# Attention, then two expert layers on one core: first q, k and v split before the branch, the attention's order planned anew, weight decoding moved later, one product's sixth block moved to its end

## The chip, the cores and the metric

The kernel runs on one core of one Trainium2 chip. The metric is the device time of one execution in microseconds, taken as the median of several runs.

## The reference, cut to what matters

Attention over 2 batches and 12 heads (448 positions, 64 channels) with a soft cap of the scores, then an expert layer that takes the maximum of three products, then a second one with a leaky rectifier.

```python
scores = cap * tanh((q @ k.T) / sqrt(64) / cap)
attn = exp(scores - max) / (sum + 1e-9)          # 2 x 12 heads, 448 x 448
x = (attn @ v)                                   # 896 tokens x 768
h = maximum(maximum(x @ w1, x @ w2), x @ w3)     # 768 -> 768, three products
y = h @ w_out                                    # 768 -> 768
g = y @ w_in;  g = max(g, 0) + alpha * min(g, 0) # 768 -> 2048
out = g @ w_out2                                 # 2048 -> 768
```

## The kernel before, in words

Every product of the expert layers is made of three matmuls: an operand is split into a high part, rounded to the matmul's short format (fp32r), and a remainder, and high times high, high times low and low times high are summed (`product`, L94 to L100). A split costs a cast (`rounded`, L82 on ACT or L84 on DVE) and a subtraction on DVE (`remainder`, L87). Weights come in a 64-bit format and are decoded by ACT and DVE in five steps (`decoded`, L102): ACT's absolute value (W0), two steps of DVE (W1, W2), ACT's cast (W3), DVE's subtraction (W4).

The attention goes over 12 pairs of heads. A pair has two units, of 4 and of 3 rows of probabilities, so there are units 0 to 23. For unit u TensorE makes two score tiles (`scores`, L252, each 6 or 3 matmuls), ACT takes tanh of each (L270) and exp of the unit (L274), and TensorE multiplies with v (`chunk_weighted`, L292, below PV u). The pairs in `FULL` use the probabilities and v unsplit, in plain fp32; for the others DVE first splits the unit's probabilities (`a_high` AH, `a_low` AL). The column sums come with PV; they are copied by ACT (`taken`, L322), sent over DRAM to invert and spread them, and a pair's result is normalised and split on DVE and ACT into `xh`, `xl`.

The order of all of this on every engine is made at build time: `fast_attention` lists the tasks with an engine, a cost, the tasks they depend on and a key (`KEYS`, L190); `planned` (L150) runs a list schedule over them, and the tasks are issued in the order that it gives and kept in it on each engine (`in_order`). Three weights of the first expert layer are decoded inside the attention, not before the units in `GATES` (L188). The score tiles have two PSUM buffers, so the scores of a tile wait for the tanh of the tile two before it. Engines run their own queue strictly in order.

Ahead of the attention the program loads `cap`, computes a flag from it on DVE, and every engine loads the flag and branches on it (L78, L665). Eleven matmuls on a constant (L76) run before the branch. The loads of the first pair's q and k (`first`, in two column cuts) are issued on SP behind the load of `cap`.

After the attention, `experts` (L535) computes h in six blocks f of 128 features, each with three weights; for f = 0 the last two of the twelve (batch, k) parts, which need the last two pairs, come at the end. Then y (L651 to L657): for each of six blocks o the two batches after one another, each over the six blocks k of h. Then `moe2` (L560): 16 blocks of g, six blocks of the output.

Of the kernel before, what the change touches and what calls it, by code (L numbers as in the profile page):

```python
# [10 lines left out]
F32 = mybir.dt.float32  # L11
# [9 lines left out]
P = 128  # L21
# [9 lines left out]
def attention_moe_moe2(ctx: ExitStack, tc: tile.TileContext, t):  # L31
# [18 lines left out]
    cap_t = const.tile([P, 1], F32, name="cap_t")  # L50
    nc.sync.dma_start(out=cap_t, in_=t["cap"].to_broadcast([P, 1]))
    cap2 = const.tile([P, 1], F32, name="cap2")
    nc.vector.tensor_tensor(out=cap2, in0=cap_t, in1=cap_t, op=ALU.mult)  # L53
    flag = const.tile([P, 1], I32, name="flag")
    nc.vector.tensor_scalar(out=flag, in0=cap2, scalar1=CAP_BOUND * CAP_BOUND, scalar2=None, op0=ALU.is_le)
    s_in = const.tile([P, 1], F32, name="s_in")
    nc.vector.reciprocal(out=s_in, in_=cap_t)
    nc.vector.tensor_scalar(out=s_in, in0=s_in, scalar1=scale, scalar2=None, op0=ALU.mult)
    alpha_t = const.tile([P, KF], F32, name="alpha_t")


    first = const.tile([P, QK], F32, name="first")
    CUT = S + P
    for cols in (slice(0, CUT), slice(CUT, QK)):
        nc.sync.dma_start(out=first[:, cols], in_=t["qk"][0, :, cols])
# [3 lines left out]
    fills = const.tile([P, 2, P], BF16, name="fills")  # L69
    for i in range(2):  # L70
        nc.gpsimd.memset(fills[:, i], float(i))

# [77 lines left out]
    def planned(tasks, start):  # L150
# [36 lines left out]

    GATES = (10, 13, 22)  # L188

    KEYS = dict(  # L190
        Lx=-8, Lv=-6, XKH=-4, XKL=-3.9, VH=-1.5, VL=-1.2, TKA=1.9, TKB=2, INV=2.2, NM=2.7, XH=2.9, XL=3.2,
        SC=-1.4, TA=-0.5, EX=0, AH=0.1, AL=0.2, PV=1.25,
    )
# [3 lines left out]
    def fast_attention(xh, xl, pools, begin):  # L197
# [6 lines left out]
        for i in range(2):  # L204
            sets["h", i] = vpool.tile([P, 4, 4 * D], F32R, name=f"vh{i}")
            sets["l", i] = vpool.tile([P, 4, 4 * D], F32R, name=f"vl{i}")
            if FULL:
                sets["f", i] = vpool.tile([P, 4, 4 * D], F32, name=f"vf{i}")

# [42 lines left out]
        def scores(i):  # L252

            p, block = CHUNKS[i]
            h, l = ops[p]
            sc = ps.tile([P, 2, 512], F32, tag="ps", name="sc")
            k0 = S + (3 if block is None else block) * P
            for m, (k_, q_) in enumerate(((h, h), (h, l), (l, h))):
# [124 lines left out]
        of = [[u for u in range(n // 2) if CHUNKS[2 * u][0] == p] for p in range(PAIRS)]  # L383
        for name in ("KIN", "QIN"):
            add((name, 0), name, 0.3 if name == "KIN" else 1.4, [], 0, lambda: None)
        for i in range(2):
            for part in "hlf" if FULL else "hl":
                add(("ONE", part, i), "Pool", 1.0, [], i, beside, part, i)
        for p in range(PAIRS):
# [4 lines left out]
            if p == 0:  # L394
                for x, (cols, dep) in enumerate(((slice(0, CUT), "KIN"), (slice(CUT, QK), "QIN"))):
                    m = cols.stop - cols.start
                    add(("XKH", 0, x), "DVE", rounding("DVE", m), [((dep, 0), 0.0)], -99 + x, qk_high, 0, cols, "DVE")
                    add(("XKL", 0, x), "DVE", low(m), [("XKH", 0, x)], -98.5 + x, qk_low, 0, cols)
            else:
                transfer(("Lx", p), 0.63, 2.6, past("XKL", p - 2, 0), s0 + KEYS["Lx"], load_qk, p)  # L400
                free = past("SC", 2 * of[p - 2][-1] + 1) if p > 1 else []
                engine, cols = ROUND["QK"], slice(0, QK)
                deps = [(("Lx!", p), 0.9)] + free
# [5 lines left out]
            transfer(("Lv", p), 1.2 if full else 0.63, 2.0, free + (ones if full else []), s0 + KEYS["Lv"], load_v, p)  # L409
            ready_v = [(("Lv!", p), 0.9)]  # L410
            if not full:
# [5 lines left out]
            for u in of[p]:  # L417
                even, m = u % 2 == 0, S * UNITS[u]
                for i in (2 * u, 2 * u + 1):
                    deps = past("SC", i - 1) + past("TA", 2 * u - 2) + past("TA", 2 * u - 1)  # L420
                    deps += [("XKL", 0, 0 if i == 0 else 1)] if p == 0 else [("XKL", p, 0)]
                    cost = 0.71 if CHUNKS[i][1] in (0, 1) else 0.6 if i % 2 == 0 else 0.8
                    add(("SC", i), "PE", cost, deps, u + KEYS["SC"] - i % 2 * 1000, scores, i)
# [11 lines left out]
                if not full:  # L435
# [4 lines left out]
                    add(("AL", u), "DVE", low(m), [("AH", u)] + free, u + KEYS["AL"], a_low, u)  # L440
                cost = (3.1 if even else 2.7) if full else (2.5 if even else 2.25)
                deps = [("EX" if full else "AL", u)] + ready_v + past("PV", u - 1)
# [17 lines left out]
            for h, name in enumerate(("NA", "NB")):  # L460
                add((name, p), "DVE", low(S), [(("DX!", p), 1.4)], s0 + KEYS["NM"], normal, p, h)
            engine = ROUND["X"]
            add(("XH", p), engine, rounding(engine, S), [("NA", p), ("NB", p)], s0 + KEYS["XH"], x_high, p, engine)
            add(("XL", p), "DVE", low(S), [("XH", p)], s0 + KEYS["XL"], x_low, p)
        for w, gate in enumerate(GATES):
            stages = begin(w)
            step = lambda stages=stages: next(stages, None)
            free = [("EX", gate)]
            transfer(("WL", w), 0.4, 4.2, [("EX", max(0, gate - 4))] + past("W2", w - 2), 1000 + w * 10, step)
            times = (("ACT", 0.8), ("DVE", 1.05), ("DVE", 1.8), ("ACT", 0.8), ("DVE", 0.9))  # L470
            for j, (engine, cost) in enumerate(times):
                deps = [(("WL!", w), 0.3)] + free + past("W4", w - 2) if j == 0 else [(f"W{j - 1}", w)]
                add((f"W{j}", w), engine, cost, deps, 1000 + w * 10, step)
        anchors = {}
        for name in planned(tasks, 3.6):
            task, args = tasks[name][4]
            task(*args)
            if name in (("EX", n // 2 - 1), ("AL", splitting[-1]), ("PV", n // 2 - 1), ("DA", PAIRS - 1)):
                anchors[name[0]] = list(nc.cur_bb.bb.instructions)[-1]
# [80 lines left out]
    def moe2(y, gh, gl, wpool, small, accumulator):  # L560
        yh, yl = y
        for f in range(KF):
# [4 lines left out]
            ng = small.tile([P, B, S], F32, tag="m", name="ng")  # L567
# [28 lines left out]
    def whole(fast):  # L596
        tag = "f" if fast else "g"
        with ExitStack() as outer:
# [43 lines left out]
            with ExitStack() as st:  # L642
                small = st.enter_context(tc.tile_pool(name=f"s{tag}", bufs=2))
                late = st.enter_context(tc.tile_pool(name=f"l{tag}", bufs=1))
                for ins in behind:
                    st.enter_context(tc.issue_after(ins))
                hs = [hidden(late, f) for f in range(KD)]
                for f in range(KD):
                    experts(f, weight, xs, hs, accumulator, small, 2 if f == 0 else 0)
                y = tuple(act.tile([P, KD, B, S], F32R, tag=f"a{h}", name=f"y{h}") for h in "hl")  # L650
                for o in range(KD):  # L651
                    wh, wl = whole_weights(wpool, t["w_out"][o])
                    acc = accumulator()
# [77 lines left out]
```

## Time and profile before

| what | value |
|---|---|
| median of 3 runs | 530.16 us (529.76 to 530.53) |
| the profiled execution, its own time | 533.62 us |
| its span, first to last instruction | 532.2 us, so 1.4 us lie around it |
| granted clock of TensorE, mean | 0.994 |
| busy: PE, DVE, ACT | 97%, 70%, 43% of the span |

A busy PE is not PE at its peak: the ends of matmuls are modelled, and spacing between the starts of matmuls says more than busy time. The profiled execution took 3.5 us longer than the median run.

### The profile page before, as it was taken

The numbers are of one execution on the slowest core, as the hardware profiler recorded it, in microseconds if no ns is written. First come the engines' busy times: TensorE is split into PE (matmuls) and PEld (weight loads), VectorE is DVE, ScalarE is ACT, GpSimd is POOL, SyncE is SP. The second block draws the span as 40 slices with busy tenths as digits, with TensorE's granted clock in tenths as the row PEclk, the third lists the DMA queues.
The fourth block names the chain that finished last, engine by engine and source line by source line (L and its number), as shares of the span: only waits on it lengthen the run. The fifth ranks groups of instructions, "written<-read, shape, count | busy, mean of one in ns | idle before, by whom it ended". The sixth has DMA issues, their size and how long they took to land.

```text
span 532.2 us, 6370 instructions
## 1 busy us (share of the span) xinstructions
PE 518.1 (97%) x2511; PEld 442.1 (83%) x2511; DVE 372.1 (70%) x482; ACT 228.9 (43%) x276; POOL 3.9 (1%) x12
## 2 busy tenths in 40 slices
PE   6999899999999999999999999999999999999994
PEld 3566466679999999999999999999999999999993
DVE  3487999748897666857667899999889555555300
ACT  5999989924333323333323433343233223223100
POOL 2000000000000000000000000000000000000000
PEclk9999999999999999999999999999999999999999
DMA  6548343135435323333322332333322354353001
GB/s 184 170 125 223 72 118 97 40 96 161 148 120 177 115 86 103 113 120 118 114 73 112 118 111 73 114 118 110 103 64 101 110 148 135 106 153 121 1 36 41
DMA packets 28262, 59.19 MB, mean 111 GB/s; under 512 B 15424, under 2 KB 18624, under 8 KB 28224
## 3 DMA queue, kind: packets, MB, share of 16 engines
q1 hardware_dynamic: 28224, 58.69, 36.1%
q8 instruction: 22, 0.36, 0.3%
q14 instruction: 16, 0.13, 0.1%
HBM read 55.85 MB, written 2.80 MB: 110 GB/s over the span
## 4 chain that ended last, share of the span: by engine, by line
PE 96%; ACT 1%; DMA 1%; DVE 0%; issue 0%; DVEq 0%; ACTq 0%
PE acc L98 26%; PE acc L99 26%; PE acc L100 26%; PE pv L311 12%; PE sc L261 6%; ACT a L270 1%; DMA cap_t<-in_cap 1%; ACT a L274 0%; ACT e L322 0%; DVE qkl L87 0%; ACT wh L82 0%; DVE qkh L84 0%; ACT ot L584 0%; DVEq L78 0%; DVE cap L53 0%
## 5 line engine op out<-in xcount | busy, mean ns | idle before, releaser
L82 ACT CAST wh<-f 128x768 fp32r<-128x768 f32 (+1 forms) x58 | 47.2, 814 | 203.7 <-PE acc L99 195.4
L87 DVE TENSOR_TENSOR wl<-f,wh 128x768 fp32r<-128x768 f32 (+1 forms) x58 | 53.7, 925 | 52.4 <-ACT wh L82 52.3
L98 PE MATMUL acc<-xh,wh 128*128 128x448 f32 x216 | 79.0, 366 | 0.0
L99 PE MATMUL acc<-xl,wh 128*128 128x448 f32 x216 | 79.0, 366 | 0.0
L100 PE MATMUL acc<-xh,wl 128*128 128x448 f32 x216 | 78.9, 365 | 0.0
L108 ACT ACTIVATE f<-raw 128x768 f32<-128x768 f32 (+1 forms) x58 | 51.2, 882 | 54.2 <-DVE wl L87 39.1
L98 PE MATMUL acc<-yh,wh 128*128 128x448 f32 x192 | 70.7, 368 | 0.0
L99 PE MATMUL acc<-yl,wh 128*128 128x448 f32 x192 | 70.7, 368 | 0.0
L100 PE MATMUL acc<-yh,wl 128*128 128x448 f32 x192 | 70.7, 368 | 0.0
L98 PE MATMUL acc<-gh,wh 128*128 128x448 f32 x192 | 70.7, 368 | 0.0
L99 PE MATMUL acc<-gl,wh 128*128 128x448 f32 x192 | 70.7, 368 | 0.0
L100 PE MATMUL acc<-gh,wl 128*128 128x448 f32 x192 | 70.7, 368 | 0.0
L118 DVE SCALAR_TENSOR_TENSOR f<-raw,f 128x768 int32<-128x768 int32 (+1 forms) x58 | 53.9, 929 | 1.7
L115 DVE SCALAR_TENSOR_TENSOR f<-raw,f 128x768 int32<-128x768 int32 (+1 forms) x58 | 53.9, 929 | 1.5
L110 DVE TENSOR_SCALAR f<-f 128x768 f32<-128x768 f32 (+1 forms) x58 | 31.6, 545 | 22.6 <-ACT f L108 22.6
L270 ACT ACTIVATE a<-sc,s_in 128x896 f32<-128x896 f32 (+1 forms) x48 | 41.9, 919 | 5.5 <-PE sc L261 5.3
L98 PEld LDWEIGHTS acc<-xh,wh 128*128 128x128 f32 x216 | 40.6, 188 | 3.8 <-issue 0.7
L99 PEld LDWEIGHTS acc<-xl,wh 128*128 128x128 f32 x216 | 40.6, 188 | 3.4 <-DVE xl L87 0.2
L100 PEld LDWEIGHTS acc<-xh,wl 128*128 128x128 f32 x216 | 40.6, 188 | 3.2
L311 PE MATMUL pv<-a,vf 128*128 128x448 f32 (+1 forms) x112 | 41.1, 557 | 0.0
L274 ACT ACTIVATE a<-a,cap_t 128x1792 f32<-128x1792 f32 (+3 forms) x28 | 39.5, 1422 | 0.5
L98 PEld LDWEIGHTS acc<-yh,wh 128*128 128x128 f32 x192 | 36.0, 188 | 3.7
(66 smaller groups left out, 725.7 us busy)
## 6 DMA issues: line engine op xcount, KB each, us to landing
raw<-in_w SPq DMA_DIRECT2D x18, 768.0 KB, 4.4
raw<-in_w_in SPq DMA_DIRECT2D x16, 768.0 KB, 4.3
raw<-in_w_out SPq DMA_DIRECT2D x12, 768.0 KB, 4.3
raw<-in_w_out SPq DMA_DIRECT2D x12, 640.0 KB, 4.0
qkd<-in_qk SPq DMA_DIRECT2D x11, 480.0 KB, 4.1
rb<-row SPq DMA_DIRECT2D x24, 112.0 KB, 3.0
out<-ot SPq DMA_DIRECT2D x12, 224.0 KB, 2.8
vf<-in_v SPq DMA_DIRECT2D x14, 128.0 KB, 4.0
```

Source lines behind the costliest of these rows:

```text
L82: nc.scalar.copy(out=hi, in_=src)
L87: nc.vector.tensor_tensor(out=lo, in0=src, in1=hi.bitcast(F32), op=ALU.subtract)
L98: nc.tensor.matmul(out, wh, xh, start=first and i == 0, stop=False)
L99: nc.tensor.matmul(out, wh, xl, start=False, stop=False)
L100: nc.tensor.matmul(out, wl, xh, start=False, stop=last and i == n - 1)
L108: nc.scalar.activation(out=f, in_=high.bitcast(F32), func=AF.Abs)
L115: nc.vector.scalar_tensor_tensor(out=fi, in0=low, scalar=29, in1=fi, op0=ALU.logical_shift_right, op1=ALU.bitwise_or)
L118: nc.vector.scalar_tensor_tensor(out=fi, in0=high, scalar=-0x40000000, in1=fi, op0=ALU.bitwise_and, op1=ALU.bitwise_or)
L261: nc.tensor.matmul(sc[:, head, :S], k_[r, k0 : k0 + P], q_[r, :S], start=m == 0, stop=m == 2)
L270: nc.scalar.activation(out=splits[i // 2][:, at : at + sc.shape[1]], in_=sc, func=AF.Tanh, scale=s_in)
L274: nc.scalar.activation(out=a, in_=a, func=AF.Exp, scale=cap_t)
L311: nc.tensor.matmul(pvs[p][:, head, :S], v_, a_[r, j], start=start, stop=stop)
```

## The change

The part ahead of the branch: `cap` is loaded from ACT's queue, so that the first cut of q and k is the first load on SP; v of the first pair is loaded into a tile of its own there, with its ones written by POOL; and DVE splits the first cut (576 columns) behind the flag's arithmetic and ahead of its own load of the flag.

```diff
-    nc.sync.dma_start(out=cap_t, in_=t["cap"].to_broadcast([P, 1]))
+    nc.scalar.dma_start(out=cap_t, in_=t["cap"].to_broadcast([P, 1]))
+    first = const.tile([P, QK], F32, name="first")
+    CUT = S + P
+    first_parts = [const.tile([P, CUT], F32R, name=f"first{part}") for part in "hl"]
+    first_v = const.tile([P, 4, 4 * D], F32, name="first_v")
+    for cols in (slice(0, CUT), slice(CUT, QK)):
+        nc.sync.dma_start(out=first[:, cols], in_=t["qk"][0, :, cols])
...
+    nc.gpsimd.memset(first_v[:, :, D : 3 * D], 1.0)
+    for h in range(2):
+        nc.sync.dma_start(out=first_v[:, :, 3 * h * D : (3 * h + 1) * D], in_=t["v"][0, :, :, h])
...
     nc.vector.tensor_scalar(out=flag, in0=cap2, scalar1=CAP_BOUND * CAP_BOUND, scalar2=None, op0=ALU.is_le)
+    nc.vector.tensor_copy(out=first_parts[0], in_=first[:, :CUT])
+    nc.vector.tensor_tensor(
+        out=first_parts[1], in0=first[:, :CUT], in1=first_parts[0].bitcast(F32), op=ALU.subtract
+    )
```

The planner: other keys, costs and gates; all that it yields is an order.

```diff
-    GATES = (10, 13, 22)
+    GATES = (10, 16, 23)
-        SC=-1.4, TA=-0.5, EX=0, AH=0.1, AL=0.2, PV=1.25,
+        XH=-2.55, XL=-3.75, SC=-4.5, TA=-0.25, EX=-28.75, AH=-3.0, AL=-12.65, PV=7.5,
-                    cost = 0.71 if CHUNKS[i][1] in (0, 1) else 0.6 if i % 2 == 0 else 0.8
+                    cost = (0.86, 0.8, 0.72, 0.8)[i % 4]
-        for name in planned(tasks, 3.6):
+        for name in planned(tasks, 5.0):
```

The second layer's temporary `ng` lies in the tiles `first` and `first_v` in turn, in place of two buffers of a pool. The first block of y takes k = 0 to 4 of both batches first, and the sixth block of h, k = 5, for both at the end:

```diff
-                    for b in range(B):
-                        terms = [((wh[:, k], wl[:, k]), tuple(h_[:, b] for h_ in hs[k])) for k in range(KD)]
-                        product(acc[:, b], terms)
+                    early = KD - 1 if o == 0 else KD
+                    for k0, k1 in ((0, early), (early, KD)):
+                        for b in range(B) if k0 < k1 else ():
+                            terms = [((wh[:, k], wl[:, k]), tuple(h_[:, b] for h_ in hs[k])) for k in range(k0, k1)]
+                            product(acc[:, b], terms, k0 == 0, k1 == KD)
```

What it moves. First PE at the start of the attention, from score tile 3 (of one head's width, `sc_192`) to PV 0; `sc` are scores, `pv` the product with v, numbers are buffers, `x4` is four matmuls. Before:

```order
L261 MATMUL sc_192<-qkh_145 128x448
L261 MATMUL sc_192<-qkl_146,qkh_145 128x448
L261 MATMUL sc_192<-qkh_145,qkl_146 128x448
L261 MATMUL sc_209<-qkh_181 128x448 x2
L261 MATMUL sc_209<-qkl_182,qkh_181 128x448 x2
L261 MATMUL sc_209<-qkh_181,qkl_182 128x448 x2
L261 MATMUL sc_218<-qkh_181 128x448 x2
L261 MATMUL sc_218<-qkl_182,qkh_181 128x448 x2
L261 MATMUL sc_218<-qkh_181,qkl_182 128x448 x2
L311 MATMUL pv_229<-a_166,vf0_138 128x448 x4
```

and now, up to the first score tile of unit 2 (`sc_220`):

```order
L270 MATMUL sc_196<-firsth_61,qkh_152 128x448
L270 MATMUL sc_196<-firstl_62,qkh_152 128x448
L270 MATMUL sc_196<-firsth_61,qkl_153 128x448
L320 MATMUL pv_202<-a_169,first_v_63 128x448 x4
L270 MATMUL sc_220<-qkh_207 128x448 x2
L270 MATMUL sc_220<-qkl_208,qkh_207 128x448 x2
L270 MATMUL sc_220<-qkh_207,qkl_208 128x448 x2
```

The score tiles 4 and 5 of unit 2 stood ahead of PV 0; now PV 0 comes right behind tile 3. Second, PE in the middle, from score tile 29 (`sc_663`, the second one of unit 14) to the first matmuls of PV 12 (`pv`, pair 6, split). Before:

```order
L261 MATMUL sc_663<-qkh_567 128x448 x2
L261 MATMUL sc_663<-qkl_568,qkh_567 128x448 x2
L261 MATMUL sc_663<-qkh_567,qkl_568 128x448 x2
L261 MATMUL sc_687<-qkh_567 128x448 x2
L261 MATMUL sc_687<-qkl_568,qkh_567 128x448 x2
L261 MATMUL sc_687<-qkh_567,qkl_568 128x448 x2
L261 MATMUL sc_700<-qkh_567 128x448
L261 MATMUL sc_700<-qkl_568,qkh_567 128x448
L261 MATMUL sc_700<-qkh_567,qkl_568 128x448
L311 MATMUL pv_707<-ah_659,vh0_136 128x448
L311 MATMUL pv_707<-al_677,vh0_136 128x448
L311 MATMUL pv_707<-ah_659,vl0_137 128x448
```

and now:

```order
L270 MATMUL sc_663<-qkh_566 128x448 x2
L270 MATMUL sc_663<-qkl_567,qkh_566 128x448 x2
L270 MATMUL sc_663<-qkh_566,qkl_567 128x448 x2
L320 MATMUL pv_680<-ah_638,vh0_144 128x448
L320 MATMUL pv_680<-al_651,vh0_144 128x448
L320 MATMUL pv_680<-ah_638,vl0_145 128x448
```

Before, tiles 30 and 31 of unit 15 stood between tile 29 and PV 12; now they come behind PV 12. Third, ACT at the same place, from exp 13 (`a_637`) to the tanh of tiles 28 and 29 (`sc_647`, `sc_663`); `e<-pv` is a copy of pair 5's products and sums, `wh<-f` the step W3 of the first weight. Before:

```order
L274 ACTIVATE a_637<-a_637,cap_t_58 128x1344
L322 COPY e_656<-pv_598 128x448
L82 CAST wh_606<-f_608 128x768
L322 COPY e_656<-pv_598 128x448
L270 ACTIVATE a_674<-sc_647,s_in_64 128x896
L270 ACTIVATE a_674<-sc_663,s_in_64 128x896
```

and now (tile 28 is `sc_654` here):

```order
L90 CAST wh_572<-f_574 128x768
L283 ACTIVATE a_640<-a_640,cap_t_58 128x1344
L331 COPY e_670<-pv_609 128x448
L279 ACTIVATE a_676<-sc_654,s_in_78 128x896
L279 ACTIVATE a_676<-sc_663,s_in_78 128x896
L331 COPY e_670<-pv_609 128x448
L283 ACTIVATE a_676<-a_676,cap_t_58 128x1792
```

W3 stands ahead of exp 13 and the second copy behind the two tanh, so that between exp 13 and the tanh of tile 28 one copy is left of three instructions. The step W0 of the second weight, which stood right behind the tanh of tile 29, now stands behind exp 16.

## Rows read from the trace of the kernel before

**Rows 1.** Stages of the span: length, then busy us (count) by engine, PEclk, DMA.

```profile
13.67:30.63 16.96, 16.96 (x77) 9.19 (x75) 9.70 (x12) 15.62 (x18) 0.00 (x0) 1.00 0.44 135
30.63:62.28 31.65, 31.65 (x165) 20.94 (x164) 26.04 (x42) 30.86 (x35) 0.00 (x0) 1.00 0.61 161
62.28:64.72 2.44, 0.37 (x5) 0.00 (x2) 2.44 (x3) 2.44 (x5) 0.00 (x0) 1.00 0.11 26
65.40:68.80 3.40, 3.40 (x11) 2.84 (x10) 3.40 (x5) 3.40 (x4) 0.00 (x0) 0.50 0.71 149
68.80:110.35 41.55, 41.55 (x200) 26.02 (x198) 34.47 (x54) 36.84 (x47) 0.00 (x0) 1.00 0.29 77
...
129.83:245.15 115.32, 115.32 (x571) 106.86 (x569) 86.14 (x105) 41.11 (x48) 0.00 (x0) 1.00 0.39 124
245.67:524.46 278.79, 278.79 (x1350) 253.23 (x1349) 190.74 (x235) 84.27 (x104) 0.00 (x0) 1.00 0.31 99
```

The columns of busy time are PE, PEld, DVE, ACT and POOL.

**Rows 2.** The chain that ended last, 0 to 16 us: start, us, what.

```profile
0.73 3.27 DMA cap_t<-in_cap
...
4.46 0.50 DVEq L78
...
5.21 0.73 DVE qkh L84
...
5.96 0.77 DVE qkl L87
...
7.54 1.91 ACT a L270 x2
9.45 1.85 ACT a L274 x2
...
13.74 2.45 PE pv L311 x6
```

**Rows 3.** Timeline of PE at the first long idle time (in brackets, with its releaser).

```profile
12.26 0.48 PE L261 MATMUL sc<-qkh 64*128 64x448 f32 x2 [1.87 <-ACT a L270]
```

**Rows 4.** The chain that ended last, 60 to 70 us: start, us, what.

```profile
62.08 0.51 ACT e L322
62.59 0.73 ACT wh L82
...
63.75 0.92 ACT a L270
```

**Rows 5.** Timeline of weight loads (PEld) and of DVE around 129 and 245 us.

```profile
129.52 0.19 PEld L99 LDWEIGHTS acc<-xl,wh 128*128 128x128 f32 x1 [0.23 <-DVE xl L87]
...
245.35 0.19 PEld L99 LDWEIGHTS acc<-hl,wh 128*128 128x128 f32 x1 [0.22 <-DVE hl L87]
...
244.21 1.09 DVE L87 TENSOR_TENSOR hl<-m,hh 128x896 fp32r<-128x896 f32 x1
```

**Rows 6.** Timeline of the head: DVE's cast of the second cut, ACT's tanh of unit 2.

```profile
6.63 0.43 DVE L84 CAST qkh<-first 128x384 fp32r<-128x384 f32 x1
...
14.10 1.91 ACT L270 ACTIVATE a<-sc,s_in 128x896 f32<-128x896 f32 x2
```

**Rows 7.** Timeline of DVE (first weight's steps, AH, AL) and of PE at PV 12.

```profile
57.18 0.56 DVE L110 TENSOR_SCALAR f<-f 128x768 f32<-128x768 f32 x1 [0.22 <-ACT f L108]
...
59.36 0.96 DVE L118 SCALAR_TENSOR_TENSOR f<-raw,f 128x768 int32<-128x768 int32 x1
...
61.63 1.08 DVE L84 CAST ah<-a 128x1792 fp32r<-128x1792 f32 x1
...
63.70 2.02 DVE L87 TENSOR_TENSOR al<-a,ah 128x1792 fp32r<-128x1792 f32 x1
...
66.90 0.57 PE L311 MATMUL pv<-ah,vh 128*128 128x448 f32 x1
```

**Rows 8.** Timeline of DVE and of weight loads at the start of g.

```profile
288.33 1.08 DVE L87 TENSOR_TENSOR yl<-acc,yh 128x896 fp32r<-128x896 f32 x1
...
289.69 0.19 PEld L99 LDWEIGHTS acc<-yl,wh 128*128 128x128 f32 x1
```

More of the change, by code (lines that the diff above doesn't have):

```diff
@@ L50, in attention_moe_moe2 @@
     cap_t = const.tile([P, 1], F32, name="cap_t")
-    nc.sync.dma_start(out=cap_t, in_=t["cap"].to_broadcast([P, 1]))
+    nc.scalar.dma_start(out=cap_t, in_=t["cap"].to_broadcast([P, 1]))
[5 more added lines that the diff above has]
+        nc.sync.dma_start(out=first[:, cols], in_=t["qk"][0, :, cols])
+    fills = const.tile([P, 2, P], BF16, name="fills")
+    for i in range(2):
+        nc.gpsimd.memset(fills[:, i], float(i))
+    nc.gpsimd.memset(first_v[:, :, D : 3 * D], 1.0)
+    for h in range(2):
+        nc.sync.dma_start(out=first_v[:, :, 3 * h * D : (3 * h + 1) * D], in_=t["v"][0, :, :, h])
     cap2 = const.tile([P, 1], F32, name="cap2")
@@ L59, in attention_moe_moe2 @@
     alpha_t = const.tile([P, KF], F32, name="alpha_t")
[L62 to L65, printed above, removed]
     nc.sync.dma_start(out=alpha_t, in_=t["alpha"])
@@ L68, in attention_moe_moe2 @@
     nc.scalar.activation(out=warm, in_=cap_t, func=AF.Tanh)
-    fills = const.tile([P, 2, P], BF16, name="fills")
-    for i in range(2):
-        nc.gpsimd.memset(fills[:, i], float(i))
     with tc.tile_pool(name="idle", bufs=1, space=PSUM) as idle:
@@ L186, in attention_moe_moe2 @@
     }
[L188 removed]
+    GATES = (10, 16, 23)
     KEYS = dict(
[L191 to L192 removed]
+        Lx=-4.5, Lv=-8.5, XKH=-24.75, XKL=22.1, VH=9.5, VL=2.05, TKA=-30.1, TKB=4.5, INV=-8.0, NM=21.0,
+        XH=-2.55, XL=-3.75, SC=-4.5, TA=-0.25, EX=-28.75, AH=-3.0, AL=-12.65, PV=7.5,
     )
@@ L207, in fast_attention @@
             if FULL:
-                sets["f", i] = vpool.tile([P, 4, 4 * D], F32, name=f"vf{i}")
+                sets["f", i] = vpool.tile([P, 4, 4 * D], F32, name=f"vf{i}") if i else first_v
         def values(p, part):
@@ L254, in scores @@
             p, block = CHUNKS[i]
-            h, l = ops[p]
+            kh, kl = first_parts if i == 0 else ops[p]
+            qh, ql = first_parts if p == 0 else ops[p]
             sc = ps.tile([P, 2, 512], F32, tag="ps", name="sc")
             k0 = S + (3 if block is None else block) * P
-            for m, (k_, q_) in enumerate(((h, h), (h, l), (l, h))):
+            for m, (k_, q_) in enumerate(((kh, qh), (kh, ql), (kl, qh))):
                 for head in range(1 if block is None else 2):
@@ L383, in fast_attention @@
         of = [[u for u in range(n // 2) if CHUNKS[2 * u][0] == p] for p in range(PAIRS)]
[L384 to L388, printed above, removed]
+        for name, cost in (("XKL", 0.4), ("QIN", 0.4), ("Lv!", 2.2)):
+            add((name, 0, 0) if name == "XKL" else (name, 0), name, cost, [], 0, lambda: None)
+        for i, (part, x) in enumerate((("f", 1), ("h", 0), ("l", 0), ("h", 1), ("l", 1))):
+            add(("ONE", part, x), "Pool", 0.6, [], i, beside, part, x)
         for p in range(PAIRS):
@@ L394, in fast_attention @@
             if p == 0:
[L395 to L398, printed above, removed]
+                cols, m = slice(CUT, QK), QK - CUT
+                add(("XKH", 0, 1), "DVE", rounding("DVE", m), [(("QIN", 0), 0.0)], -99, qk_high, 0, cols, "DVE")
+                add(("XKL", 0, 1), "DVE", low(m), [("XKH", 0, 1)], -98, qk_low, 0, cols)
             else:
-                transfer(("Lx", p), 0.63, 2.6, past("XKL", p - 2, 0), s0 + KEYS["Lx"], load_qk, p)
+                transfer(("Lx", p), 0.5, 1.6, past("XKL", p - 2, 1 if p == 2 else 0), s0 + KEYS["Lx"], load_qk, p)
                 free = past("SC", 2 * of[p - 2][-1] + 1) if p > 1 else []
                 engine, cols = ROUND["QK"], slice(0, QK)
-                deps = [(("Lx!", p), 0.9)] + free
+                deps = [(("Lx!", p), 1.9)] + free
                 add(("XKH", p, 0), engine, rounding(engine, QK), deps, s0 + KEYS["XKH"], qk_high, p, cols, engine)
@@ L408, in fast_attention @@
             ones += [] if full else past("ONE", "l", kin.index(p) % 2)
-            transfer(("Lv", p), 1.2 if full else 0.63, 2.0, free + (ones if full else []), s0 + KEYS["Lv"], load_v, p)
-            ready_v = [(("Lv!", p), 0.9)]
+            if p:
+                free = free + (ones if full else [])
+                transfer(("Lv", p), 1.2 if full else 0.5, 1.5 if full else 1.0, free, s0 + KEYS["Lv"], load_v, p)
+            ready_v = [(("Lv!", p), 1.7)]
             if not full:
@@ L440, in fast_attention @@
                     add(("AL", u), "DVE", low(m), [("AH", u)] + free, u + KEYS["AL"], a_low, u)
-                cost = (3.1 if even else 2.7) if full else (2.5 if even else 2.25)
+                cost = (3.2 if even else 2.1) if full else (2.65 if even else 2.0)
                 deps = [("EX" if full else "AL", u)] + ready_v + past("PV", u - 1)
@@ L460, in fast_attention @@
             for h, name in enumerate(("NA", "NB")):
-                add((name, p), "DVE", low(S), [(("DX!", p), 1.4)], s0 + KEYS["NM"], normal, p, h)
+                add((name, p), "DVE", 0.65, [(("DX!", p), 1.4)], s0 + KEYS["NM"], normal, p, h)
             engine = ROUND["X"]
@@ L468, in fast_attention @@
             free = [("EX", gate)]
-            transfer(("WL", w), 0.4, 4.2, [("EX", max(0, gate - 4))] + past("W2", w - 2), 1000 + w * 10, step)
-            times = (("ACT", 0.8), ("DVE", 1.05), ("DVE", 1.8), ("ACT", 0.8), ("DVE", 0.9))
+            transfer(("WL", w), 0.4, 3.0, [("EX", 6 + 5 * w)] + past("W2", w - 2), 1000 + w * 10, step)
+            times = (("ACT", 0.8), ("DVE", 1.2), ("DVE", 1.87), ("ACT", 0.8), ("DVE", 0.9))
             for j, (engine, cost) in enumerate(times):
-                deps = [(("WL!", w), 0.3)] + free + past("W4", w - 2) if j == 0 else [(f"W{j - 1}", w)]
+                deps = [(("WL!", w), 1.5)] + free + past("W4", w - 2) if j == 0 else [(f"W{j - 1}", w)]
                 add((f"W{j}", w), engine, cost, deps, 1000 + w * 10, step)
         anchors = {}
-        for name in planned(tasks, 3.6):
+        for name in planned(tasks, 5.0):
             task, args = tasks[name][4]
@@ L561, in moe2 @@
         yh, yl = y
+        spare = first[:, : B * S], first_v.rearrange("p c n -> p (c n)")[:, : B * S]
+        spare = [x.rearrange("p (b s) -> p b s", b=B) for x in spare]
         for f in range(KF):
@@ L566, in moe2 @@
                 product(acc[:, b], [((wh[:, k], wl[:, k]), (yh[:, k, b], yl[:, k, b])) for k in range(KD)])
-            ng = small.tile([P, B, S], F32, tag="m", name="ng")
+            ng = spare[f % 2]
             nc.vector.tensor_scalar(
```

## The prediction

> **What bounds the kernel now.** I read the page's busy shares first: TensorE (PE) 97%, DVE 70%, ACT 43%. PE is the bound, so a change is worth what it takes out of PE's own time: idle time, a lower clock, or wider spacing of matmuls. Then a table of stages [rows 1], whose columns show where PE's time is poorer than elsewhere, and for each such place the chain of waits or the timeline. The reader is to see four losses.
>
> (a) The head. The branch waits for a flag; the load of `cap` takes 3.27 us and lands at 4.0, the flag load ends at 4.96, and only then DVE splits the first cut (0.73 + 0.77 us), so that the first tanh starts at 7.54 and PE's first product with v at 13.7 [rows 2]. Between them PE is idle 1.87 us, waiting for a tanh to free a score buffer [rows 3].
>
> (b) The middle. In 62.28 to 64.72 PE is busy 0.37 of 2.44 us [rows 1]: 2.07 us idle. The chain there is four ACT instructions in a row: a copy, a weight cast (W3, 0.73), another copy, and at 63.75 the tanh of score tile 28, which frees the buffer that PE's tile 30 waits for [rows 4].
>
> (c) Right behind it, 65.40 to 68.80, PEclk is 0.50 [rows 1], the 1.2 GHz level, after the idle stretch; the stages on both sides have 1.00. Work of 3.40 us at half clock costs 1.7 us.
>
> (d) The expert layers. From 129.83 to 245.15 there are 569 weight loads, one for each matmul, in 115.32 us: 0.2027 us from one to the next. From 245.67 to 524.46 it is 278.79/1349 = 0.2067 [rows 1]. PEclk is 1.00 in both and the matmuls have one shape (128x448). The 0.0040 us times 1349 are 5.4 us. What lies between the two stages is a wait of 0.22 us: PE's weight load at 245.35 waits for `hl`, the remainder of h's sixth block, ready at 245.30 [rows 5]. A like wait for `xl` at 129.52 (0.23 us) [rows 5] lies ahead of narrow spacing, so a wait alone doesn't decide it.
>
> **The change part by part.** The sum is made against the profiled execution, 533.62 us (span 532.2 and 1.4 around it). The median of the runs is 530.16, 3.5 us less; I can't see where, and subtract the same saving from both.
>
> Head. DVE now splits the first cut at 4.46, ahead of its flag load, where before it began at 5.21 [rows 2]: the first score tile and the first tanh come 0.75 us earlier, at 6.8, if the cut has landed by then. But DVE's flag load (0.50) and branch (0.25) now come behind the split, so the second cut is cast from about 4.46 + 1.50 + 0.75 = 6.7, against 6.63 before: no gain for score tile 1, and the second tanh comes at some 8.25 instead of 8.45. The order shows PV 0 ahead of score tiles 4 and 5, so PE fills its 1.87 us of idle with PV 0: it starts at about 10.2, when half of exp 0 is done (8.25 + 0.96 for tanh, 0.93 for half of the exp [rows 2]), instead of 13.7. That is not a gain of 3.5 us: tile 4 then stands behind PV 0's eight matmuls, 3.2 us at the 2.45 for six [rows 2], and ends at 10.2 + 3.2 + 0.6 = 14.0, about when ACT took its tanh before, 14.10 [rows 6]. And from there to 30.63 ACT is busy 15.62 of 16.96 us [rows 1], so it, not PE, limits what PE's lead is worth: at most the 1.34 us that it was idle. I take a gain of 0.5; bounds are a gain of 1.9 (all of PE's idle time) and a loss of 0.75 (the flag late by as much as the split was moved). That `cap` is issued on ACT's queue I price at nothing, since ACT otherwise waits for that same load; it hides behind the wait, and costs what it is issued later, below 0.5 (the flag load, the nearest small transfer of a queue).
>
> By the Trainium skill ("DMA: Bandwidth & Descriptors", section on queues, rings and completion order), an engine with work from two queue rows takes turns between them packet by packet, so that `cap`, now in a row of its own, shares the engines with the first cut instead of being ahead of it on one ring. No row of before shows two rings there; by the rule the flag could come later, and the term would go to its lower bound, 0.75 us of loss.
>
> Middle. W3 moves ahead of exp 13 and a copy behind the tanh; of the 62.08 to 63.75 ahead of the tanh [rows 4] one copy (0.51) is left. So tanh 28 comes about 1.2 us earlier by its own queue; and on PE, PV 12 stands ahead of tile 30, so tile 30 isn't wanted at 62.3 any more. What is late next is PV 12, which needs AL 12. Before, AL 12 was done at 63.70 + 2.02 = 65.7 [rows 7] and PV 12 began at 66.90 [rows 7]; now PE comes to it right behind tile 29, at about 61.4 (62.3 less the 0.5 of the head and 0.4 of smaller shifts). In DVE's order there now stand, ahead of AL 12, the four weight steps (0.56 + 0.56 + 0.96 + 0.96 = 3.0), two products, AH (1.08) and one cast, but no longer the 1.15 us of the q, k remainder; and the weight steps, which began at 57.18 behind ACT's W0 [rows 7], come earlier, since W0 does. Counted from there AL 12 ends at 61.5 to 62. I take a wait of 0.4 us in place of the 2.07, and no drop of the clock: −2.07 − 1.7. Bounds: a gain of all of it, and none (AL 12 as late as before, 65.7).
>
> The rest of the attention, 68.80 to 110.35, has PE busy throughout [rows 1]; W0 to W4 of the second and third weight go to later gates, where DVE (34.47 of 41.55) and ACT (36.84) have 5 to 7 us of room. No gain; 0.2 us of small waits. The loads that start with these weights move with them.
>
> Expert layers. With k = 5 of both batches last in y's first block, PE has 30 matmuls (6.1 us) instead of 15 (3.0) between the end of h and the first use of `hl`; before, the first of them at `hl` was due 3.0 us behind that end and came 0.2 later, so the wait goes with some 2.8 us to spare. The `xl` of the last pair comes about 0.7 us earlier, since less stands ahead of it, so the 0.23 us at 129.52 go too: −0.4. If no wait disturbs the run of matmuls, I expect the spacing of 0.2027 to last to the end: −5.4. Bounds: nothing, and a loss of 2.6 us (131.5 us from 110.35 to about 241.9, some 649 matmuls, widened by 0.0040).
>
> The Trainium skill ("TensorE: Matmul & The Clock Gate", section "Wait — 56ns, not 53.3ns?") gives the start-to-start time of warm matmuls as their columns over 2.4 GHz plus some 2.5 ns, for 448 columns an estimate of 0.189 us. By it spacing hangs on the columns alone, nothing would be won here, and the time would be that of the first rival below. The trace disagrees in part: one shape, one clock, two spacings.
>
> `ng` in the tiles of `first` costs nothing: the tiles' last readers are done 170 us before. The splits themselves keep their sizes.
>
> Sum: −0.5 − 2.1 − 1.7 − 0.4 − 5.4 + 0.6 (0.4 + 0.2 of new waits) = −9.5. From 533.6 that is 524.1; from the median 530.16 it is 520.7 us.
>
> **The rivals.**
> Spacing is not kept. The narrow spacing may end for another reason than the wait, as `xl`'s wait did not end it. Then the term is 0: 530.16 − 4.1 = 526.1. Variants: wide from g on, where `yl` is ready at 289.41 and used at 289.69 [rows 8], only 0.28 us apart, less if matmuls go faster: some 220 matmuls stay narrow, 525.2; wide from the start of the experts: 528.7. For it: one cause seen once; against it: the change of spacing lies exactly at the wait.
>
> The wait moves to PV 12. AL 12 is as late as W1 to W2 make it; PE then idles as long as before and the clock falls again: 2.1 + 1.7 − 0.4 are lost of the sum, with the spacing kept 524.1. For it: PE's need moves from 66.9 to 61.4, by 5.5 us, and AL 12 must follow. Against: of the 31.65 us from 30.63 to 62.28 DVE works 26.04 [rows 1], so there is room.
>
> Both fail: 530.16 − 0.5 − 0.4 + 0.6 = 529.9.
>
> Slower. DVE keeps strict order, so if the first weight's W1 stands waiting for its data, AL 12 stands behind it, and PE at PV 12 behind that. With wide spacing this decides from a wait of 4.1 + 1.1 = 5.2 us on; with narrow, from 10.6. At 6 us the time would be 532. For it: transfers hold the DMA engines 0.61 of the time up to 62.28 and 0.71 behind it [rows 1]. Against: before, W1's idle time of 0.22 us was ended by ACT's W0, not by a transfer [rows 7].
>
> **How the numbers follow.** Chances: both gains 0.43 (520.7); spacing not kept 0.33 (525.2 to 528.7); the wait at PV 12 with the spacing kept 0.11 (524.1); both fail 0.07 (529.9); slower 0.06 (532). The forecast is the likeliest, 520.7; its own range is 518.5 to 522.5 (head bounds of −1.4 and +1.25, half a us for small waits). The range of 8 in 10, 518.0 to 528.5, takes in the first three cases and leaves out the last two and the ends. A measurement can tell about 0.2%, 1.1 us (529.1 to 531.2), from no change. The first three cases are all faster, 0.87; both fail is the same, 0.07; slower 0.06.
>
> **What the profile after would show.** Head right: the split before the flag load, PV 0 at about 10.2, PV 4 near 30.1. Middle right: no idle time of PE above 1 us and PEclk 1.00 from 55 to 70. Experts right: first matmul of h near 105.8 (110.35 − 4.3 − the small shifts + 0.6), no wait of a weight load for `hl` or `xl`, 0.2027 us from weight load to weight load until the end. Wrong: PE waiting for `al` on DVE at PV 12; a spacing of 0.2067 from h's sixth block, from g, or from the start; `cap` landing after 4.5.

## The result, and the profile after

The changed kernel took 524.62 us (median of 6 runs, 523.97 to 534.28) beside 530.41 us of the kernel before (529.76 to 532.70): a ratio of 0.9863, 95% interval 0.9818 to 0.9908, in which one slow run, 534.28, is left out. That is 5.8 us less, where 9.5 were forecast. The profiled executions are 525.13 us (span 523.4) and 533.62 (span 532.2): 8.5 us apart. So most of the sum is found again between the two profiles, and not between the medians; the experiments had to say why.

The stages of the changed kernel (length, busy time and count of PE, PEld, DVE, ACT and POOL, granted clock, DMA) answer to [rows 1]:

```profile
10.11:29.62 19.51, 19.02 (x86) 10.01 (x86) 9.67 (x13) 17.50 (x21) 0.00 (x0) 1.00 0.61 173
29.62:62.22 32.60, 32.19 (x167) 21.03 (x165) 28.54 (x39) 31.96 (x37) 0.00 (x0) 1.00 0.57 155
66.77:67.72 0.95, 0.00 (x1) 0.01 (x1) 0.92 (x2) 0.51 (x1) 0.00 (x0) 1.00 0.05 2
67.72:107.34 39.62, 39.62 (x192) 24.86 (x192) 35.37 (x53) 37.05 (x47) 0.00 (x0) 1.00 0.35 82
107.34:238.80 131.46, 131.46 (x650) 121.87 (x649) 96.69 (x125) 43.93 (x53) 0.00 (x0) 1.00 0.40 126
238.81:515.45 276.64, 276.64 (x1367) 256.66 (x1366) 194.09 (x238) 86.81 (x107) 0.00 (x0) 1.00 0.32 103
```

PEclk is 1.00 in each of these stages. The expert layers begin at 107.34 instead of 110.35. From 238.81 on there are 1366 weight loads in 276.64 us, 0.2025 us each, against 0.2067 in the same part before. The last matmul of the program starts at 515.85, where before it started at 524.46 (the end of the last stage of [rows 1]):

```profile
515.85 0.36 PE L108 MATMUL acc<-gh,wl 128*128 128x448 f32 x1
```

So the expert layers, first to last matmul, took 408.5 us instead of 414.1.

The head, in the timeline of DVE (start, length, line, operation; in brackets the idle time ahead and what ended it):

```profile
4.64 0.16 DVE L66 TENSOR_TENSOR cap<-cap_t 128x1 f32<-128x1 f32 x1 [4.64 <-DMA cap_t<-in_cap]
...
4.98 0.45 DVE L69 CAST firsth<-first 128x576 fp32r<-128x576 f32 x1
5.46 0.76 DVE L70 TENSOR_TENSOR firstl<-first,firsth 128x576 fp32r<-128x576 f32 x1
6.26 0.62 DVE L92 CAST qkh<-first 128x384 fp32r<-128x384 f32 x1
```

`cap` comes at 4.64, 0.6 later than the 4.03 of before, and the first split begins at 4.98, 0.2 earlier than the 5.21 of [rows 2]. And PE's timeline, with the products with v that the prediction spoke of, against [rows 2] and [rows 7]:

```profile
10.11 3.25 PE L320 MATMUL pv<-a,first_v 128*128 128x448 f32 x8
...
29.62 0.47 PE L320 MATMUL pv<-ah,vh 128*128 128x448 f32 x1
...
62.22 0.47 PE L320 MATMUL pv<-ah,vh 128*128 128x448 f32 x1
...
66.40 0.36 PE L320 MATMUL pv<-ah,vh 128*128 128x448 f32 x1
67.72 0.47 PE L320 MATMUL pv<-al,vh 128*128 128x448 f32 x1 [0.96 <-DVE al L95]
```

PV 0 starts at 10.11 and PV 4 at 29.62; PV 12 comes without an idle time behind tile 29, at 62.22; then PV 13 waits 0.96 us for AL 13, which DVE works at from 66.12 for 1.54 us:

```profile
64.82 0.85 DVE L92 CAST ah<-a 128x1344 fp32r<-128x1344 f32 x1
65.58 0.61 DVE L360 TENSOR_TENSOR rb<-e,rb 64x448 f32<-64x448 f32 x1
66.12 1.54 DVE L95 TENSOR_TENSOR al<-a,ah 128x1344 fp32r<-128x1344 f32 x1
```

### The profile page after: what moved, and what is told of

The parts are those of the page before. It is cut to its first block, busy times and chain, and to the rows that moved or that the text cites. A ratio compares the mean times of both kernels' runs of the same rounds, so it can differ in the third digit from the quotient of the medians.

```text
span 523.4 us, 6377 instructions
## 1 busy us (share of the span) xinstructions
PE 512.1 (98%) x2511; PEld 441.5 (84%) x2511; DVE 371.9 (71%) x482; ACT 227.8 (44%) x276; POOL 3.6 (1%) x12
## 4 chain that ended last, share of the span: by engine, by line
PE 88%; DVE 3%; ACT 2%; DMA 2%; issue 1%; SPq 0%; ACTq 0%; DVEq 0%
PE acc L106 26%; PE acc L108 26%; PE acc L107 26%; PE pv L320 7%; PE sc L270 3%; DMA rc<-e 2%; DVE al L95 1%; ACT a L279 1%; ACT a L283 1%; DVE ah L92 1%; DVE qkl L95 0%; DVE qkh L92 0%; DMA row<-rc 0%; DVE rb L360 0%; ACT e L331 0%
## 5 line engine op out<-in xcount | busy, mean ns | idle before, releaser
L106 PEld LDWEIGHTS acc<-gh,wh 128*128 128x128 f32 x192 | 36.1, 188 | 2.8
L107 PEld LDWEIGHTS acc<-yl,wh 128*128 128x128 f32 x192 | 36.1, 188 | 2.8
```

Source lines behind the costliest of these rows:

```text
L106: nc.tensor.matmul(out, wh, xh, start=first and i == 0, stop=False)
L107: nc.tensor.matmul(out, wh, xl, start=False, stop=False)
```

## The experiments

**Is a profile the kernel?** The kernel before was run again, unchanged.

> The kernel before, unchanged, profiled and timed once more: is the spacing of its matmuls the same in every execution? My theory (the wait for hl switches it): 0.2067 us from h's sixth block on in this profile too, and a half-clock stretch behind the idle time at 62 us; median 530.2. Rival (the spacing belongs to the execution, not to the order): another stage or no stage is wide, and the executions scatter by up to 8 us (2000 matmuls times 0.0040).

Measured 531.51 us (12 runs, 529.93 to 537.47), ratio 0.9997 (0.9954 to 1.0039). The windows of its profile, an execution of 535.71 us:

```profile
13.53:16.94 3.41, 3.41 (x9) 1.57 (x6) 2.25 (x4) 3.38 (x5) 0.00 (x0) 0.50 0.78 249
64.36:67.30 2.94, 0.00 (x1) 0.00 (x2) 2.94 (x3) 2.94 (x6) 0.00 (x0) 1.00 0.33 67
68.15:71.55 3.40, 3.37 (x11) 3.04 (x10) 3.40 (x5) 3.40 (x4) 0.00 (x0) 0.50 0.61 158
132.50:247.71 115.21, 115.21 (x571) 106.78 (x569) 85.70 (x105) 41.04 (x48) 0.00 (x0) 1.00 0.37 124
248.22:527.00 278.78, 278.78 (x1350) 253.23 (x1349) 190.76 (x235) 84.37 (x104) 0.00 (x0) 1.00 0.31 99
```

The spacing switches at `hl` here too (115.21/569 = 0.2025, then 278.78/1349 = 0.2067). But there are two stretches at half clock instead of one, and the idle time in the middle is 2.94 instead of 2.07 us. And the executions fall in two groups. In the sessions of the experiments the kernel before ran 92 times, this experiment's runs among them: 47 took 527.87 to 532.80 us (median 530.56; below, the short group), 45 took 533.15 to 537.99 (median 535.94; the long group). The gap between them is small, so an execution near 533 can be on either side. Their mean granted clock is the same (medians 0.990 and 0.989), so the clock does not part them. The groups are 5.4 us apart, which is what 1349 matmuls at 0.0040 us make. One order with two outcomes, as the rival has it, is what the times suggest; the two traces of this kernel are both of the long group.

**The order of k alone**, in the kernel before:

```diff
-                    for b in range(B):
-                        terms = [... for k in range(KD)]
-                        product(acc[:, b], terms)
+                    early = KD - 1 if o == 0 else KD
+                    for k0, k1 in ((0, early), (early, KD)):
+                        for b in range(B) if k0 < k1 else ():
+                            terms = [... for k in range(k0, k1)]
+                            product(acc[:, b], terms, k0 == 0, k1 == KD)
```

> The kernel before with only the order of k in y's first block changed (k = 5 of both batches last). My theory: the weight load no longer waits for hl, the spacing stays at 0.2027 to the end of the program, and 5.4 + 0.2 us go: 524.6. Rival (spacing not tied to that wait): the wait goes, the spacing is as before, 530.0.

Measured 530.19 us (12 runs, 528.44 to 531.82), ratio 0.9951 (0.9917 to 0.9985). Its windows, with the same places as above:

```profile
14.02:17.43 3.41, 3.41 (x5) 1.48 (x5) 2.09 (x3) 3.38 (x4) 0.00 (x0) 0.50 0.70 246
64.68:67.68 3.00, 0.01 (x2) 0.00 (x0) 3.00 (x4) 3.00 (x6) 0.00 (x0) 1.00 0.25 49
68.64:72.04 3.40, 3.40 (x9) 3.09 (x10) 3.40 (x5) 3.40 (x4) 0.00 (x0) 0.50 0.60 164
...
248.22:520.00 271.78, 271.78 (x1343) 251.91 (x1342) 191.14 (x236) 84.26 (x104) 0.00 (x0) 1.00 0.31 102
```

271.78/1342 = 0.2025 to the end, no weight load that waits for `hl`, and none of 12 executions in the long group, where about half of the kernel before are. That fits a wait that has to do with the switch (the last experiment below limits how far); but the time is that of the short group of before (530.56), not 524.6. By that, the 5.4 us are won only in an execution that would have been long.

**The order of k put back**, in the changed kernel (the same diff, reversed).

> The changed kernel with only the order of k in y's first block put back. My theory: the wait for hl of about 0.2 us is back, and from it on the spacing is 0.2067: 524.1 + 5.5 = 529.6. Rival: narrow all the same, 524.3.

Measured 526.30 us (6 runs, 523.78 to 531.77), ratio 0.9892 (0.9829 to 0.9955). The wait is back, and the spacing of the profiled execution (523.78 us) is narrow all the same, 268.67/1326 = 0.2026:

```profile
241.01 0.19 PEld L107 LDWEIGHTS acc<-hl,wh 128*128 128x128 f32 x1 [0.22 <-DVE hl L95]
...
241.33:510.00 268.67, 268.67 (x1327) 249.03 (x1326) 190.70 (x235) 84.29 (x104) 0.00 (x0) 1.00 0.32 103
```

Two of the other five lie 5 us (529.20) and 8 us (531.77) above; a switch at `hl` would make 5, but neither was traced. So the wait alone doesn't switch the spacing; that it lets it switch is not shown.

**The changed kernel again**, twice.

> The changed kernel, unchanged, beside the others on the same chip. My theory: narrow spacing from start to end in this profile too, 524.1. Rival (spacing belongs to the execution): wide in some stage, up to 532 for a wide execution.

> The changed kernel once more, as the measure for the next one. In three of its profiles so far a weight load waits for xl of pair 10 some 5.8 us into the expert layers, or just misses to. My theory (each such short wait may switch the spacing): most executions 524 to 527, some near 533 (2000 matmuls times 0.0040 more). Rival (the spacing belongs to the chip's state): the share of long executions is that of the kernel before in the same minutes.

Measured 526.40 us (524.27 to 533.19), ratio 0.9854 (0.9794 to 0.9914), and 524.05 us (523.53 to 531.68), ratio 0.9847 (0.9792 to 0.9902). Both profiles are narrow throughout. In the first one the attention ends 2.2 us later than in the profile shown above, and the reason stands in the head: DVE's cast of the second cut took 1.97 us instead of 0.62, PE stood still 1.36 us for it, and a half-clock stretch followed.

```profile
6.14 1.97 DVE L92 CAST qkh<-first 128x384 fp32r<-128x384 f32 x1
...
8.17 0.47 PE L270 MATMUL sc<-firsth,qkh 64*128 64x448 f32 x2 [1.36 <-DVE qkh L92]
...
8.60:11.90 3.30, 3.29 (x15) 2.30 (x12) 2.96 (x5) 2.33 (x3) 0.00 (x0) 0.50 0.99 279
```

DMA engines are 0.99 busy in that stretch. Over the three sessions the changed kernel ran 18 times: 15 took 523.53 to 527.27 (median 524.27), three took 531.68 to 534.28. The three have a mean granted clock of 0.996 to 0.997, like the others, so the clock did not make them long; they lie 7.4 to 10.0 us above the median of the others, more than the 5.4 of a switch at `hl`. Wide spacing of all 2016 matmuls of the expert layers would make 8.1 (an estimate, 2016 times 0.0040).

**The head put back in part** (`cap`'s queue and the split; q, k and v of the first pair are still loaded ahead of the branch, and the planner's order stays):

```diff
-    nc.scalar.dma_start(out=cap_t, in_=t["cap"].to_broadcast([P, 1]))
+    nc.sync.dma_start(out=cap_t, in_=t["cap"].to_broadcast([P, 1]))
...
-    nc.vector.tensor_copy(out=first_parts[0], in_=first[:, :CUT])
-    nc.vector.tensor_tensor(out=first_parts[1], ...)
...
+            nc.vector.tensor_copy(out=first_parts[0], in_=first[:, :CUT])
+            nc.vector.tensor_tensor(out=first_parts[1], ...)
         for name in planned(tasks, 5.0):
```

> The changed kernel with its head put back: cap loaded first on SP's queue, the split of the first cut behind DVE's flag load and branch; the planner's order as in the changed kernel. My theory (the head is worth 0.5 to 1 us): the attention ends 0.7 us later, 525 us. Rival (the head carries the gain): PE idles again for some 2 us before PV 0 and a half-clock stretch follows, 527 to 528.

Measured 529.61 us (6 runs, 524.74 to 534.49), ratio 0.9879 (0.9799 to 0.9959). The median says little: three executions are near 525 (524.74, 525.10, 526.63), three near 533. In the profiled one (524.74) PV 0 starts 0.4 us later than in the changed kernel and the expert layers begin at 106.44, with no half-clock stretch:

```profile
10.48 3.25 PE L316 MATMUL pv<-a,first_v 128*128 128x448 f32 x8
...
6.00:106.44 100.44, 98.69 (x484) 61.38 (x484) 79.95 (x115) 94.37 (x112) 1.98 (x4) 1.00 0.47 128
```

So `cap`'s queue and the early split bring PV 0 forward by 0.4 us; on the whole time they are worth nothing that these runs can tell, as the changed kernel's own profiles begin the expert layers at 105.9 to 109.5. That PV 0 comes at 10 and not at 13.7 is the order's doing (PV 0 ahead of tile 4), which this kernel keeps.

**New gates alone**, in the kernel before (`GATES = (10, 16, 23)`).

> The kernel before with only GATES changed to (10, 16, 23). PE's order is that of before, W3 of the first weight no longer stands between exp 13 and the tanh of tile 28. My theory (those ACT instructions make the idle time at 62 us): PE's idle time there falls from 2 to 3 us to 1 or less, no half-clock stretch behind it; 530.2 - 1.5 - 1.7 = 527. Rival (PE's order makes it: tiles 30 and 31 ahead of PV 12): idle time and clock stay, 530.

Measured 529.50 us (12 runs, 527.55 to 534.54), ratio 0.9936 (0.9894 to 0.9979); nine are below 530.2, with a median of 529.1, and three between 532.9 and 534.5. The wait for `hl` is still there, and the profiled execution (527.55) keeps narrow spacing behind it, 273.00/1348 = 0.2025:

```profile
245.46 0.19 PEld L99 LDWEIGHTS acc<-hl,wh 128*128 128x128 f32 x1 [0.22 <-DVE hl L87]
...
246.00:519.00 273.00, 273.00 (x1349) 253.40 (x1348) 190.55 (x234) 84.25 (x104) 0.00 (x0) 1.00 0.32 101
```

PE's idle time in the middle fell to 1.85 us and no half-clock stretch followed it, but one stayed in the head:

```profile
13.88:17.29 3.41, 3.41 (x5) 1.41 (x5) 1.18 (x3) 3.38 (x4) 0.00 (x0) 0.50 0.89 303
64.30:66.15 1.85, 0.01 (x2) 0.00 (x0) 1.85 (x2) 1.85 (x4) 0.00 (x0) 1.00 0.09 21
66.15:70.00 3.85, 3.83 (x21) 3.22 (x21) 3.79 (x5) 3.82 (x4) 0.00 (x0) 1.00 0.91 246
```

My expectation named the wrong ACT instruction: W3 still stands there, as ACT's timeline shows,

```profile
63.51 0.52 ACT L322 COPY e<-pv 128x448 f32<-128x448 f32 x1
63.92 0.83 ACT L82 CAST wh<-f 128x768 fp32r<-128x768 f32 x1
64.66 0.53 ACT L322 COPY e<-pv 128x448 f32<-128x448 f32 x1
65.08 1.92 ACT L270 ACTIVATE a<-sc,s_in 128x896 f32<-128x896 f32 x2
```

between exp 13 and the tanh of tile 28. What makes the idle time longer or shorter seems to lie ahead of it: in the profile of before run again, ACT stood still for a product of DVE,

```profile
54.41 0.57 ACT L82 CAST xh<-rb 128x448 fp32r<-128x448 f32 x1 [0.99 <-DVE rb L351]
```

and PE's idle time was 2.94 us. With k = 5 last and with k = 5 first (below) the same cast waits 0.94 and 0.84, and PE is idle 3.00 both times; here, and in the first profile of before, it waits for nothing, and PE's idle time is 1.85 and 2.07. Since the first profile of before has the old gates, the new ones are not what ended that wait.

**Old gates** (`GATES = (10, 13, 22)`), and then **all of the planner's old numbers** (KEYS, costs, GATES), in the changed kernel.

> The changed kernel with GATES put back to (10, 13, 22). PE's order then has tiles 30 and 31 ahead of PV 12 again. My theory: PE idles 2 us or more near 62 us, and a half-clock stretch follows; 524.3 + 2.1 + 1.7 = 528. Rival (the new keys and costs, not the gates, end the stall): 524.5.

> The changed kernel with the planner's keys, costs and gates of before; the head and the order of k in y's first block stay changed. My theory: like the one with the old gates alone, 528, since those numbers only move the instructions around unit 14. Rival (the new keys and costs carry the gain): 530 or more. Rival (the head carries it): 525.

Measured 529.17 us (12 runs, 527.03 to 532.08), ratio 0.9890 (0.9856 to 0.9925), and 529.17 us (12 runs, 528.27 to 530.90), ratio 0.9915 (0.9881 to 0.9949). The size was about as expected and the place was not. With the old gates PE has no idle time near 62 us; two of its waits come while the second weight is decoded (71 to 94 us) and one behind it, in PE's timeline:

```profile
82.36 0.47 PE L270 MATMUL sc<-qkh 64*128 64x448 f32 x2 [1.10 <-ACT a L279]
...
85.48 0.47 PE L320 MATMUL pv<-al,vh 128*128 128x448 f32 x1 [1.15 <-DVE al L95]
...
99.56 0.47 PE L270 MATMUL sc<-qkh 64*128 64x448 f32 x2 [0.83 <-ACT a L279]
```

These waits add up to 3.1 us. Both profiles (530.29 and 530.04) also have a cast of the second cut of 2.00 and 1.97 us and a half-clock stretch in the head, as one profile of the changed kernel above, so the time of these two executions is not the planner's numbers alone. In the kernel with all the old numbers PV 0 stands early all the same, ahead of the next score tile:

```profile
9.42 3.16 PE L320 MATMUL pv<-a,first_v 128*128 128x448 f32 x4
12.51 0.47 PE L270 MATMUL sc<-firsth,qkh 64*128 64x448 f32 x2
```

So it is not the new keys, costs or gates that put it there. What this kernel shares with the changed one is v of the first pair, loaded ahead of the branch; SP issues it at 1.66 in the changed kernel (first row) and at 7.29 in the kernel before (second row). No run put that load back, so this cause is likely and not shown.

```profile
1.66 1.33 SPq L64 DMA_DIRECT2D first_v<-in_v  x2
...
7.29 2.69 SPq L228 DMA_DIRECT2D vf<-in_v  x4
```

New keys and costs without the new gates win nothing that these runs can tell (529.17 both). By medians of different sessions, the gates alone are worth 1.5 us (530.56 to 529.1 between the short groups), beside the new keys and costs 4.9 (529.17 to 524.27): the numbers seem to work together.

**A part put off.** In the changed kernel a weight load (PEld), 5.7 us into the expert layers, comes some 0.1 us late, as the `xl` of pair 10 that it loads is ready on DVE only at 113.0 (112.37 + 0.63):

```profile
112.72 0.19 PEld L106 LDWEIGHTS acc<-xh,wh 128*128 128x128 f32 x1
113.05 0.19 PEld L107 LDWEIGHTS acc<-xl,wh 128*128 128x128 f32 x1
...
112.37 0.63 DVE L95 TENSOR_TENSOR xl<-rb,xh 128x448 fp32r<-128x448 f32 x1
```

The part that needs it was moved behind the other two weights:

```diff
+                mine = some
+                if late and w == 0:
+                    mine = some[:-1] if n == 0 else parts[0][-1:] + some
-                for b, k in some:
+                for b, k in mine:
```

> The changed kernel with one product of the first expert weight put off: the part of pair 10 (batch 1, k = 3) comes 1.4 us or more later, behind the other weights, so that no weight load waits for its xl. My theory: no execution near 533 any more, all 524 to 527. Rival: a like share of executions near 533 as in the changed kernel.

> The changed kernel with the head put back (three of six executions were near 533 there, the others near 525) and with the part of pair 10 put off. My theory (the long executions come from the short wait for xl of pair 10, which is gone): one group, 524.5 to 527, and no execution above 530. Rival (the put-off part has nothing to do with it): again some executions near 533. On the head: if it is worth nothing that can be measured, the median is that of the changed kernel's short executions, 524 to 525.

Measured 525.23 us (6 runs, 524.01 to 526.51), ratio 0.9874 (0.9823 to 0.9924), and with the old head 524.82 us (6 runs, 524.57 to 525.47), ratio 0.9825 (0.9770 to 0.9880). None of these 12 executions is above 526.51; of the 18 of the changed kernel and the six with the old head, six were above 531. That fits my theory, and with six runs each it is no more than an indication: no long execution of the changed kernel was caught in a trace, so where it becomes long is not shown. Neither version beats the short executions of the changed kernel (median 524.27); they may only be steadier.

**k = 5 first**, in the kernel before, to make PE stand still for `hl`.

> The kernel before with k = 5 first in y's first block, so that PE stands still some 3 us for hl and starts anew. If any wait may switch the spacing: executions in two groups, 533.2 and 538.6. If only a short wait does, one that comes between two matmuls: one group at 530.1 + 3.0 = 533.1. A half-clock stretch behind the wait may add 1.7.

Measured 530.90 us (12 runs, 529.21 to 536.80), ratio 0.9993 (0.9956 to 1.0030). The experiment missed its aim: outside the attention a scheduler sets the order at build time, and it put other blocks ahead, so that the wait is as short as before:

```profile
249.72 0.19 PEld L99 LDWEIGHTS acc<-hl,wh 128*128 128x128 f32 x1 [0.21 <-DVE hl L87]
```

Behind that wait the profiled execution (532.22) is narrow to the end, 273.00/1348 = 0.2025:

```profile
250.00:523.00 273.00, 273.00 (x1348) 253.04 (x1348) 190.50 (x235) 84.24 (x104) 0.00 (x0) 1.00 0.32 101
```

What the experiment leaves is one long execution of 12, where the kernel before had 45 of 92, at a wait of like length. With the wait gone (k = 5 last) there were none of 12, which these counts can't tell from one. So not the length of the wait alone decides; whether it was the wait or the other order of the products that took the long executions away is not shown, and whether a long wait switches the spacing stays open.

## Why the prediction was right in its direction and too large

**Spacing (−5.4).** In the profile it came as forecast: no wait for `hl` or for the last pair's `xl`, 0.2025 to the end, and the expert layers 5.6 us shorter. (The two waits themselves were taken for 0.4 and are 0.2: the loads waited 0.22 and 0.23, but on PE one step from matmul to matmul became 0.31 instead of 0.20 at each.) The step that failed is the one on the median: "3.5 us less; I can't see where, and subtract the same saving from both". The profile of before that I had was an execution of the long group, and the three runs that made the median (529.76 to 530.53) were of the short one; if the spacing had not switched there, this term is 0. That the short group keeps narrow spacing is read from other kernels: of all 14 profiles the two of the kernel before (533.62 and 535.71) are wide, and the twelve others (523.78 to 532.22) narrow to the end, among them the ones with k = 5 last (530.47) and k = 5 first (532.22), whose attention is that of before, and three with a wait for `hl`. A short execution of the kernel before itself was not traced. By this the 3.5 us that I could not place are 5.4 less for the spacing and some 2 more for the attention (an estimate from the later profiles, below). The rule of the Trainium skill ("TensorE: Matmul & The Clock Gate", section "Wait — 56ns, not 53.3ns?"), which gives matmuls issued back to back a time by their columns (by the prediction's estimate 0.189 us here), does not fit these runs, in which every matmul has a weight load of its own: one shape at one clock had 0.2027 and, in both profiles of the kernel before, also 0.2067.

**Attention (−0.5 − 2.1 − 1.7 + 0.6 = −3.7).** Between the two first profiles 3.0 us (110.35 to 107.34): the idle time of 2.07 and the half-clock stretch are gone, PV 13's wait of 0.96 took the place of the 0.4 that I allowed at PV 12 (in the two later profiles of the changed kernel this wait is 1.35 and nothing), and there are two smaller ones, 0.49 and 0.41, near 28 and 30 us. But that profile of before was a mild one: later ones, of it and of it with k = 5 last, have 2.94 and 3.00 us idle and a second half-clock stretch at 14 us, behind the idle time of 1.9 us in the head [rows 3], and start the expert layers at 113.0 and 113.4; the changed kernel's start at 105.9 to 109.5. So in the median the attention is worth about 6 us (an estimate), more than forecast, and by it that is all that the median shows: 530.56 to 524.27 between the short groups, 6.3 us.

Both errors have one root, one execution taken for the kernel, and they went in opposite directions. That the measured time still lies in the stated range of 518.0 to 528.5 is in part luck: the 5.4 us that the median did not have were partly made up by an attention worth more than I forecast.

**Head.** PV 0 at 10.11 (forecast 10.2), PV 4 at 29.62 (forecast near 30.1, before 30.63): up to there 1.0 us was gained, not 0.5. The cause was misjudged: PV 0's place in the order brings it, the early split only 0.4 us. The flag load and branch of 0.75 us that I put between the split and the cast of the second cut did not show: the cast begins at 6.26, right behind the split, and not at 6.7. `cap` from ACT's queue came at 4.49 to 4.64 in the seven profiles of kernels with the new head and at 3.99 to 4.09 in the seven where SP loads it first, issued at 0.73 or 0.74 either way. This is the direction of the Trainium skill ("DMA: Bandwidth & Descriptors", the section on queues, rings and completion order), by which an engine takes turns between two queue rows; the price was 0.4 to 0.6 us, below the 0.75 of my lower bound, and since the split came ahead of the flag load, PE still won a little.

**The rivals.** The wait at PV 12 did not come; it came one product later, at PV 13, in some profiles, and the clock did not fall behind it. Of the first rival (spacing not kept), no trace of the changed kernel shows wide spacing; but in the median its sum, 526.1 with the spacing worth nothing, was nearer to the 524.62 than mine.

## What to carry to other kernels

Before a term is subtracted from a median, ask whether the median has it: a profile is one execution, and here two of four terms were not the same in the next one. A saving that removes a chance of a bad outcome shows in the spread and not in the median: here 45 of 92 executions of the kernel before were in its long group, and three of 18 of the changed kernel in its own. And an idle time of PE is to be priced with the half-clock stretch that may follow it: in the kernel before, these together were worth more than the wait that one sees.

## What the runs showed of the hardware that I had not expected

A run of matmuls of one shape (128x448) at full granted clock has two steady spacings, 0.2025 to 0.2027 (by the stretch that one counts) and 0.2067 us. A switch was seen in traces only at a weight load that waited 0.22 us for its operand, in two of the five traces with such a wait at `hl`; in the other three the spacing stayed narrow across a wait of 0.21 or 0.22. What decides between them is open.

Around the 1.87 to 1.89 us of idle time in the head, ending near 12.3 us, a half-clock stretch began at 11.6 to 14.0 us in the four later profiles of the kernel before and its variants (in the one with k = 5 first it lasted 6.8 us and not 3.4), and none did in the first profile of before; with 1.35 or 1.36 us of idle time in the head, in three profiles with the new head, one came too. After 1.85 us in the middle none followed, after 2.07, 2.94 and 3.00 one did. So idle time of like length costs some 1.7 us more in one execution and nothing more in another.
